# Awaiting the last stores behind the closing barrier instead of ahead of it

## The chip, the cores and the metric

The kernel runs on one core of a Trainium2 chip. The core has five engines that run their own instruction streams and meet only through semaphores: TensorE (PE), VectorE (DVE), ScalarE (ACT), GpSimd (POOL) and SyncE (SP), which issues most of the DMA transfers. The metric is device time in microseconds (us) of one execution. The profile of one execution gives a span, from its first to its last recorded instruction, beside the time of that same execution.

## The reference

The input is one sequence `x` of 2048 rows by 1024 columns in bfloat16. Two attention blocks are computed from it and mixed row by row by a gate:

```python
g = sigmoid((x * gate_w).sum(-1))
a = A(x, A_wqkv, A_wo)     # linear attention, 32 heads of 32: phi(q) (phi(k)^T v) / (phi(q) sum phi(k)), then @ wo
b = B(x, B_wqkv, B_wo)     # local attention: each row sees 8 rows back in steps of 2, softmax, then @ wo
out = g * a + (1 - g) * b
```

`phi(t)` is `t + 1` for positive `t`, otherwise `exp(t)`, plus 1e-6. Both blocks begin with a projection of 1024 to 3072 columns.

## The kernel before, in words

The kernel is written as a list of operations, each with an engine, a cost, the memory it reads and writes and a priority. A planner in `Prog.schedule` (line 122) orders them on each engine by these costs and priorities, and `Prog.emit` (line 208) turns the plan into the engines' instruction streams with the semaphore waits that the dependencies need. All matrix products run in tiles of 128 rows by 512 columns with eight accumulating steps. Projections for both blocks come first, then the local attention, the totals of the linear attention, and at last the output: for each tile `t` of 128 rows, `final(t)` (line 1736) multiplies block B's result with its output matrix on TensorE (line 1747), VectorE adds the gated result of block A (line 1751), and a DMA stores the tile (line 1757). Two output buffers, `o0` and `o1`, take turns.

The last tile is split into three column parts, 0 to 512, 512 to 768 and 768 to 1024. Each part is stored on its own: the first two by SyncE, the third by ScalarE. Each store raises a semaphore when its data has landed; which one follows from the buffer and the first column: `c_out0_0`, `c_out1_0`, `c_out1_512` and `c_out1_768`.

Near the end every engine runs `tail` (line 1820). It waits for a flag, computed on VectorE from the data (line 1798), which says whether the fast formulas are safe for this input; it loads the flag into a register (line 1823) and branches on it (line 1824). If the flag is 0, the engine finishes its planned operations, waits for everything, and then runs a second, general program (`general_path`), whose instructions stand in the stream between the branch and the other arm. If the flag is not 0, which is what happens with these inputs, the engine jumps to the other arm (line 1830). How much planned work lies behind the branch differs by engine: `BACK` keeps the last 19 us of the plan behind it on SyncE, 14 us on VectorE and 30 us on ScalarE; TensorE and GpSimd have none there and branch after all their work.

In that other arm SyncE, once its last stores are issued, waits for the completion semaphores that no later operation has waited for (`P.last`, line 260). They are the four named above. Then the arms join, and the block that holds all five streams closes at line 1836. Its close is a barrier: SyncE, ScalarE, TensorE and VectorE each execute a DRAIN, which counts the engine as arrived; GpSimd, having executed its own, waits for all four, and then lets every engine through with a second semaphore step. Behind the barrier nothing of the kernel follows.

Of the kernel before, what the change touches and what calls it, by code (L numbers as in the profile page):

```python
# [1116 lines left out]
def build_kernel(nc, A_x, A_wqkv, A_wo, B_x, B_wqkv, B_wo, gate_w, out):  # L1117
# [698 lines left out]
    P, flag_op = best[:2]  # L1816
# [3 lines left out]
    def tail(e, eng, rest):  # L1820
        reg = e.alloc_register("fast_ok")
        e.wait_ge(*flag_op.val)
        e.reg_load(reg, flag[0:1, 0:1])
        with e.If_eq(reg, 0):
            rest()
            for s, v in P.final + [(P.esem[x], n) for x, n in P.counts.items() if n]:
                e.wait_ge(s, v)
            for th in progs[eng]:
                th(e)
        with e.Else():  # L1830
            rest()
            if eng == "sp":
                for s, v in P.last:
                    e.wait_ge(s, v)

    with nc.Block() as block:
        P.emit(block, tail, flag_op)
    es_g.__exit__(None, None, None)
    return P


def bass_gated_mix__linear_attn_block__sliding_local_dilated__prompt_kernel(nc, A_x, A_wqkv, A_wo, B_x, B_wqkv, B_wo, gate_w, out):
    return build_kernel(nc, A_x, A_wqkv, A_wo, B_x, B_wqkv, B_wo, gate_w, out)
# [28 lines left out]
```

## Time and profile before

| | |
|---|---|
| median of 4 runs | 483.16 us (482.53 to 483.67) |
| the profiled execution's own time | 482.88 us |
| its span, first to last recorded instruction | 481.1 us |
| TensorE matmul busy | 471.4 us, 98% |
| VectorE busy | 281.3 us, 58% |
| ScalarE busy | 146.6 us, 30% |
| GpSimd busy | 6.2 us, 1% |
| granted TensorE clock | 1.000 |

A busy time counts computing instructions alone: register loads, branches, semaphore waits and the issuing of DMAs are not counted, and in answers on single lines they carry the engine's name with a q (SPq, PEldq). PE means matmuls, PEld the loads of their stationary operand. A releaser is what ended an engine's wait. A line with "x2" stands for two instructions. For a DMA, "us to landing" is counted from its issue to its semaphore. Answers on single lines give starts to a tenth of a microsecond; a narrower window places an instruction more closely.

### The profile page before, as it was taken

Reading aid. Unit: us, or ns where it says so; the run is one execution under the profiler, and the core shown is the slowest. Engines: PE = TensorE matmul, PEld = TensorE weight load, DVE = VectorE, ACT = ScalarE, POOL = GpSimd, SP = SyncE. Lnnn points to the kernel's source line nnn. Section 1 sums busy time; section 2 is a strip of 40 time slices with the busy share of each in tenths; the row PEclk is TensorE's granted clock in tenths of the full one; section 3 lists DMA queues with packets and bytes.
Section 4 is the critical chain, followed back from the end, with each engine's and each line's share of the span. In section 5 each row is a group of like instructions: output and inputs, shape, how many; then the busy total and the mean of one; then the engine's idle time right before and its main releaser. Section 6 shows DMA issues by size and latency. Waiting matters only on the chain.

```text
span 481.1 us, 10169 instructions
## 1 busy us (share of the span) xinstructions
PE 471.4 (98%) x4354; PEld 224.0 (47%) x4403; DVE 281.3 (58%) x578; ACT 146.6 (30%) x234; POOL 6.2 (1%) x38
## 2 busy tenths in 40 slices
PE   8999999999999999999999999999999999999997
PEld 3444444444444544545454455444444444444443
DVE  3212337888587788556737565597588136643434
ACT  2111111135333345435434335255542130111000
POOL 4000000000000000000000000000000000000000
PEclk9999999999999999999999999999999999999999
DMA  8999991132014337432313457720194019830212
GB/s 210 250 213 313 351 361 62 50 111 82 1 35 140 88 102 146 95 70 66 78 43 86 99 130 165 227 45 2 19 249 128 0 20 249 213 23 2 89 68 90
DMA packets 72951, 57.39 MB, mean 119 GB/s; under 512 B 37953, under 2 KB 60865, under 8 KB 72898
## 3 DMA queue, kind: packets, MB, share of 16 engines
q1 hardware_dynamic: 72210, 56.07, 44.4%
q8 instruction: 36, 0.59, 0.5%
q10 hardware_dynamic: 688, 0.59, 0.4%
q14 instruction: 17, 0.14, 0.1%
HBM read 34.49 MB, written 13.76 MB: 100 GB/s over the span
## 4 chain that ended last, share of the span: by engine, by line
PE 98%; issue 1%; DVE 0%
PE ps_all L1344 80%; PE ps_all L1747 11%; PE ps_all L1464 2%; PE ps_all L1499 2%; PE ps_all L1588 1%; PE ps_all L1383 1%; PE ps_all L1692 0%; PE ps_all L1664 0%; DVE o L1751 0%; DVE warm L1290 0%
## 5 line engine op out<-in xcount | busy, mean ns | idle before, releaser
L1344 PE MATMUL ps_all<-w,xT 128*128 128x512 bf16 x934 | 206.7, 379 | 3.1 <-issue 2.5
L1344 PE MATMUL ps_all<-xT,w 128*128 128x512 bf16 x750 | 165.6, 379 | 2.0 <-issue 1.6
L1344 PEld LDWEIGHTS ps_all<-w,xT 128*128 128x128 bf16 x960 | 92.3, 98 | 110.6 <-DMA xT<-in_A_x_dram 0.8
L1344 PEld LDWEIGHTS ps_all<-xT,w 128*128 128x128 bf16 x768 | 74.1, 98 | 89.5 <-issue 1.3
L1747 PE MATMUL ps_all<-w,qT 128*128 128x512 bf16 (+1 forms) x260 | 55.4, 372 | 0.2
L1747 PEld LDWEIGHTS ps_all<-w,qT 128*128 128x128 bf16 x264 | 25.8, 98 | 29.7
L1355 DVE TENSOR_SCALAR e<-e 128x512 bf16<-128x512 bf16 x64 | 18.6, 291 | 32.1 <-ACT e L1353 17.1
L1478 ACT ACTIVATE E<-ps_all 128x1824 bf16<-128x1824 f32 (+1 forms) x18 | 30.4, 1688 | 18.9 <-PE ps_all L1499 18.9
L1375 DVE CAST vst<-ps_all 128x512 bf16<-128x512 f32 x16 | 11.1, 694 | 41.7 <-PE ps_all L1344 41.7
L1751 DVE SCALAR_TENSOR_TENSOR o<-ps_all,gm,xT 128x512 bf16<-128x512 f32 (+1 forms) x25 | 18.0, 728 | 21.2 <-PE ps_all L1747 21.1
L1353 ACT ACTIVATE e<-ps_all 128x512 bf16<-128x512 f32 x32 | 19.1, 597 | 31.4 <-PE ps_all L1344 31.4
L1351 ACT ACTIVATE e<-ps_all 128x512 bf16<-128x512 f32 x32 | 19.1, 597 | 26.0 <-PE ps_all L1344 24.8
L1302 DVE TENSOR_TENSOR mx<-mx,kT 128x1024 bf16<-128x1024 bf16 x32 | 21.0, 687 | 9.1 <-ACT kT L1376 9.0
L1516 DVE TENSOR_TENSOR ot<-ps_all,rs 128x480 bf16<-128x480 f32 (+1 forms) x54 | 25.9, 507 | 0.0
L1302 DVE TENSOR_TENSOR mx<-mx,qT 128x1024 bf16<-128x1024 bf16 x32 | 21.1, 687 | 7.2 <-ACT qT L1379 7.1
L1376 ACT ACTIVATE az<-ps_all 128x512 bf16<-128x512 f32 x23 | 13.8, 600 | 36.3 <-PE ps_all L1344 36.3
L1376 ACT ACTIVATE vst<-ps_all 128x512 bf16<-128x512 f32 x16 | 9.6, 600 | 47.4 <-PE ps_all L1344 47.4
L1376 ACT ACTIVATE kT<-ps_all 128x512 bf16<-128x512 f32 x21 | 12.5, 597 | 36.8 <-PE ps_all L1344 36.8
L1379 ACT ACTIVATE qT<-ps_all 128x512 bf16<-128x512 f32 x19 | 11.3, 597 | 35.3 <-PE ps_all L1344 35.3
L1515 DVE RECIPROCAL rs<-ps_all 128x15 f32<-128x15 f32 (+1 forms) x54 | 9.4, 203 | 21.2 <-PE ps_all L1499 19.3
L1357 DVE SCALAR_TENSOR_TENSOR pk<-ps_all,e 128x512 bf16<-128x512 f32 x32 | 21.7, 680 | 0.1
L1379 ACT ACTIVATE xT<-ps_all,g 128x512 bf16<-128x512 f32 x10 | 6.9, 688 | 45.1 <-PE ps_all L1344 45.1
(73 smaller groups left out, 276.2 us busy)
## 6 DMA issues: line engine op xcount, KB each, us to landing
rb<-rc_hbm SPq DMA_DIRECT2D x32, 256.0 KB, 5.6
w<-in_A_wqkv_dram SPq DMA_DIRECT2D x6, 1024.0 KB, 9.1
v<-vB_hbm SPq DMA_DIRECT2D x36, 132.0 KB, 2.7
vB_hbm<-vst SPq DMA_DIRECT2D x32, 132.0 KB, 5.4
w<-in_B_wqkv_dram SPq DMA_DIRECT2D x4, 1024.0 KB, 8.3
xn<-in_A_x_dram SPq DMA_DIRECT2D x16, 256.0 KB, 2.7
out_dram<-o SPq DMA_DIRECT2D x15, 256.0 KB, 2.2
oB_hbm<-ot SPq DMA_DIRECT2D x36, 96.0 KB, 2.0
```

The lines of the kernel that those rows point to most:

```text
L1302: P.op("dve", lambda e, m=m, op=op: e.tensor_tensor(m[:, 0:n], m[:, 0:n], src, op), 0.08 + n / 1920.0, reads=[m.all(), reg], writes=[m.all()],
L1344: last = e.matmul(bank.ap(), lhs(dc), rhs(dc), start=(dc == 0), stop=(dc == 7))
L1351: P.op("act", lambda e: e.activation(e_[:, :], bank.ap(), ACT.Exp), act(512), reads=[bank.iv], writes=[e_.all()])
L1353: P.op("act", lambda e: e.activation(e_[:, :], bank.ap(), ACT.Exp, accum_out=qe[:, col:col + 1]), act(512) + 0.1, reads=[bank.iv], writes= ...
L1355: P.op("dve", lambda e: e.tensor_scalar(e_[:, :], e_[:, :], 1.0, 1e-6, op0=ALU.min, op1=ALU.add), 0.25, reads=[e_.all()], writes=[e_.all()])
L1357: P.op("dve", lambda e: e.scalar_tensor_tensor(out=dst, in0=bank.ap(), scalar=0.0, in1=e_[:, :], op0=ALU.max, op1=ALU.add), dps(512), read ...
L1376: fa = lambda e: e.activation(dst, src(), ACT.Copy)
L1379: fa = lambda e: e.activation(dst, src(), ACT.Copy, scale=scale)
L1478: P.op("act", lambda e: e.activation(E[:, 0:32 * nq].rearrange("p (j q) -> p j q", j=4), ps[:, 4:8, 0:8 * nq], ACT.Exp), act(32 * nq), rea ...
L1516: P.op("dve", lambda e, r=r, src=src, dst=dst, m=m: e.tensor_tensor(dst, src()[:, :, 0:32], r[:, 0:m, None].to_broadcast([128, m, 32]), AL ...
L1747: last = e.matmul(bank.ap(0, f1 - f0), qT[:, dc, t * 128:(t + 1) * 128], ws[3][:, dc, f0:f1], start=(dc == 0), stop=(dc == 7))
L1751: P.op("dve", lambda e, bank=bank, o_=o_, t=t, n=n, i0=i0, i1=i1, tgt=tgt, c0=c0: e.scalar_tensor_tensor(out=o_[:, i0 * 128:i1 * 128].rear ...
```

## The change

Three lines leave the arm of the conditional in which SyncE waits for the completion of the last stores, and two lines with the same waits come after the block has closed. Those waits are still executed by SyncE alone. The block's close, and so the barrier, comes ahead of them in SyncE's stream.

```diff
         with e.Else():
             rest()
-            if eng == "sp":
-                for s, v in P.last:
-                    e.wait_ge(s, v)
 
     with nc.Block() as block:
         P.emit(block, tail, flag_op)
+    for s, v in P.last:
+        nc.sync.wait_ge(s, v)
     es_g.__exit__(None, None, None)
     return P
```

In the built program SyncE's four waits take two event-wait instructions and the wait of a branch before the change, and two event-wait instructions after it, two semaphores to each. The streams of the other four engines hold the same instructions in the same order.

## The prediction

> **What bounds the kernel now.** I read three things in order: the chain that ended last (what sets the span), then its last stretch in order of time, then every instruction of the lines that the change touches.
>
> The page's chain, by engine, and the chain's end by time (start, length, what):
>
> ```profile
> PE 98%; issue 1%; DVE 0%
> ```
>
> ```profile
> 469.81 8.24 PE ps_all L1747 x46
> 478.04 0.02 issue
> 478.07 0.48 DVE o L1751
> ```
>
> TensorE carries the kernel to 478.04 us, one VectorE addition to 478.55, and there the chain stops. The span is 481.1, so 481.1 - 478.55 = 2.6 us stand behind the last computation. No page row charges them to anybody; only the queue entries of the single lines show them. The change lies wholly inside these 2.6 us.
>
> The last three stores, as the DMA issues between 477 and 480 us (size, us to landing), and what SyncE waited for from 475 us on (total, times, longest):
>
> ```profile
> out_dram<-o SPq DMA_DIRECT2D x1, 128.0 KB, 2.7
> out_dram<-o SPq DMA_DIRECT2D x1, 64.0 KB, 2.9
> out_dram<-o ACTq DMA_DIRECT2D x1, 64.0 KB, 1.8
> ...
> SPq L1834 <- DMA out_dram<-o: 1.6, 1, 1.6
> ```
>
> The 64 KB store that SyncE issues at 477.7 takes 2.9 us to land: 480.6. ScalarE's, issued at 478.58, is there at 478.6 + 1.8 = 480.4. SyncE's own issue lasts 1.25 us, to 478.96, and from then it waits 1.6 us for a landing.
>
> Then each instruction of the touched lines (count, ns min/median/max, first and last start):
>
> ```profile
> L1824 PEldq COMPARE_BRANCH  x1: 3744/3744/3744, 476.3 to 476.3; - x1
> ...
> L1834 SPq EVENT_SEMAPHORE  x2: 17/22/28, 480.6 to 480.7; - x2
> ...
> L1830 SPq COMPARE_BRANCH  x1: 37/37/37, 480.7 to 480.7; - x1
> ...
> L1836 POOLq EVENT_SEMAPHORE  x2: 17/17/17, 481.0 to 481.0; - x2
> L1836 POOLq DRAIN  x1: 114/114/114, 433.8 to 433.8; - x1
> L1836 DVEq DRAIN  x1: 524/524/524, 478.1 to 478.1; - x1
> L1836 ACTq DRAIN  x1: 152/152/152, 479.0 to 479.0; - x1
> L1836 PEldq DRAIN  x1: 73/73/73, 480.1 to 480.1; - x1
> L1836 SPq DRAIN  x1: 13/13/13, 480.9 to 480.9; - x1
> L1836 SPq EVENT_SEMAPHORE  x1: 17/17/17, 481.1 to 481.1; - x1
> ```
>
> Line 1836 is the closing barrier. Each engine arrives with its DRAIN: GpSimd at 433.8, VectorE at 478.1 (done 478.60), ScalarE 479.0, TensorE 480.1, SyncE last at 480.9. GpSimd collects the arrivals and releases all. By narrowing the window to hundredths I place SyncE's steps: first wait of line 1834 at 480.60 to 480.61, second at 480.67 to 480.68, branch (line 1830) at 480.74 to 480.75, DRAIN at 480.91 to 480.92, GpSimd's two steps at 480.95 to 480.96 and 481.03 to 481.04, SyncE through the release at 481.08 to 481.09. So today the order is landing, then waits, branch and barrier, one after another. The surprise is TensorE: its last matmul starts at 477.76 and its arrival is 480.06, because its branch on the flag takes 3.7 us, from 476.26 to 480.01.
>
> **What the Trainium skill says.** "Perfetto Trace Analysis", section Sequencer-only Instruction (DRAIN, etc): the recorded time is the execution alone; the wait ahead of it and the spread of the semaphore behind it are not recorded. The trace agrees: entries of 13 to 28 ns stand 43 to 170 ns apart, so I price steps from start to start. The same page, section DMA Instruction — HWDGE (DVE, Sync): the semaphore of a store is written only after its last data write is confirmed, which can take surprisingly long into HBM; here ScalarE's 64 KB take 1.8 us. "Runtime: NRT & Kernel Launch", section Instruction fetch mechanics: a taken branch whose target isn't in the loaded window waits for a fetch. TensorE's 3.7 us branch agrees: the trace has a 16 KB instruction packet between 477.5 and 477.6 us, inside it. The same page, section The ~15µs preamble/postamble breakdown: behind the kernel the runtime has all engines wait for one another again. No view here shows that part; I use it only to say who ends the run.
>
> **The change part by part.**
>
> *Removed:* two event waits and a wait carried by the branch, in SyncE's branch of the conditional. Four completion semaphores are awaited: both output buffers and the two halves of the last tile.
>
> *Added:* the same four in two event waits behind the barrier, on SyncE alone. No matmul, vector operation or transfer changes, and the order of all engines' instructions is otherwise the same. Until the last store's issue ends at 478.96 nothing can differ, so the first 479 us cost zero, with no cover needed.
>
> *Moved, step 1: SyncE arrives early.* After 478.96 it has only its branch and DRAIN left, 480.745 to 480.925 today, some 0.2 us. It arrives near 479.2 instead of 480.92. The DRAIN might wait for transfers in flight; ScalarE's says no: at 479.0 it took 0.15 us, with its own store landing at 480.4.
>
> *Step 2: the barrier now waits for TensorE.* Arrivals: VectorE 478.60, ScalarE 479.15, SyncE 479.2, TensorE 480.06 + 0.07 = 480.14. From the last arrival to SyncE's release takes 481.085 - 480.925 = 0.16 us today, so release at 480.30, and SyncE stands at its first wait by about 480.35.
>
> *Step 3: the waits end as today.* The landing shows at 480.605; the second wait starts 0.07 us later and lasts 0.03: done at 480.70. Queued behind the waits on SyncE is only the program's end, and no other engine waits for it. The barrier is thus hidden under the store's landing with 480.605 - 480.35 = 0.25 us to spare. Without that cover (TensorE 0.25 us or more later) the gain shrinks by every further microsecond of lateness.
>
> *Sum.* The last record falls from 481.14 (TensorE's release, 481.09 + 0.05) to 480.70: -0.44 us, made of branch, DRAIN and barrier passage leaving the path. The other four engines are released at 480.3 instead of 481.1: -0.8, of use only if one of them, not SyncE, decides the run's end.
>
> The profiled execution took 482.88 us for a span of 481.1; 1.78 us lie around it. I assume they stay: 480.70 + 1.78 = 482.48 (481.14 + 1.74 before). The median of the four runs is 483.16, 0.28 above the profiled one, so against it 483.16 - 0.44 = 482.7.
>
> *Unknown cost:* what the runtime does in the 1.78 us. Lower end: nothing gained, if the end hangs on something unmoved. Upper end: 0.8, if it hangs on the four released engines. A loss isn't excluded by this either; it is bounded below. I take 0.44, because SyncE is last to finish on both sides and an end that waits for all engines waits for it.
>
> **The rivals.**
>
> *The end is set elsewhere: no change, 483.16.* For: the trace still has an instruction packet of 16 KB between 480.7 and 480.8, of the same queue as TensorE's, so an engine may be fetching its closing code whatever SyncE does. Against: it begins before today's release and nothing shows anybody waiting for it.
>
> *The four released engines decide: -0.8, 482.4.* For: TensorE's stream is the slowest at the end already. Against: SyncE's last wait would have to end nothing.
>
> *A little slower: TensorE arrives last.* If its branch took not 3.7 but over 4.5 us, it would arrive after 480.9, where SyncE arrives today. Then the barrier ends at the same moment in both kernels, and the changed one has the two event waits still to run behind it: 2 x 0.07 = 0.14 us, giving 483.3. It decides from a TensorE arrival about 0.8 us later than seen; between 0.25 and 0.6 the gain shrinks through zero. Only one execution shows the branch, so its spread is unknown.
>
> *Much slower: SyncE's new waits fall on code not yet fetched.* A stall like TensorE's 3.7 us would give up to 486.4 when nothing hides it. Against: SyncE's branch at 459.1 is followed by two 8 KB instruction packets by 462.5, which already hold the arm and its end; the next two on that queue, between 463 and 477, come after VectorE's own branch at 464.8. SyncE's stream hardly changes length.
>
> *It doesn't do what it says:* stores that land ahead of the barrier's end would leave waits of zero, and SyncE's release would again be the last record. The 0.25 us above speak against it.
>
> **How the numbers follow.** Chances: the forecast (0.44 gained) 0.58, no change 0.17 (the last rival included), 0.8 gained 0.14, a little slower 0.07, much slower 0.04. A measurement of this kernel can tell about 0.2% from no change, 0.97 us: under 482.2 or over 484.1. No mechanism above gains that much; the largest, 482.4, is 0.2 short, and the four runs alone scatter from 482.53 to 483.67, so a little of the two gaining cases spills over: faster 0.15. Slower takes the stall and a trace of scatter: 0.05. The rest, 0.80, is within. The range for 8 in 10 takes in 482.4, 483.16 and 483.3, with some 0.4 of scatter at the low end and 0.2 at the high one, where cases are rarer: 482.0 to 483.5. The stall is left out.
>
> **What would show it.** Right: SyncE's DRAIN near 479.2; TensorE's the last arrival, near 480.1; GpSimd's two steps near 480.2; SyncE's release before its event waits, and those at 480.6 and 480.7 as the last records; a span of 480.7. Step 1 is wrong if SyncE's DRAIN lasts until 480.4 or more; step 2 if another engine's arrival is last; step 3 if the release comes after the landing. A span of 480.7 with an unchanged run time says that the end is set outside the span. A second long branch, or an instruction packet ahead of SyncE's waits, would make the forecast wrong.

## The result, and the profile after

The changed kernel takes 482.42 us in the median of 40 runs (481.76 to 483.05), the kernel before 482.96 us in 60 runs. The ratio is 0.9988, with a 95% interval of 0.9983 to 0.9992: 0.58 us faster, between 0.39 and 0.82. The forecast was 482.7 us, 0.44 us faster than the 483.16 it started from.

The single profiled executions hide this: 482.77 us after against 482.88 before, and a span of 481.1 us in both. The chain's end tells why (start, length, what):

```profile
3 pieces in order of time: start us, us, what
473.85 4.78 PE ps_all L1747 x30
478.63 0.02 issue
478.65 0.48 DVE o L1751
```

The last addition ends at 479.14 us, where it ended at 478.55 before: this one execution reached the tail 0.59 us later. That lies in the 478 us that the change does not touch, and within the scatter: the runs of one kernel lie some 1.3 us apart. Behind the last addition the kernel before needed 2.59 us to its last record and 4.33 to the end of the run; the changed one needed 2.01 and 3.63. What is to be compared is the tail, and across runs, not the two spans.

The closing barrier of the changed kernel is on line 1833, its waits on line 1836. Each entry is count, ns min/median/max, first and last start:

```profile
L1824 PEldq COMPARE_BRANCH  x1: 3824/3824/3824, 476.8 to 476.8; - x1
...
L1833 POOLq EVENT_SEMAPHORE  x2: 17/17/17, 480.8 to 480.9; - x2
...
L1833 DVEq DRAIN  x1: 524/524/524, 478.7 to 478.7; - x1
L1833 SPq DRAIN  x1: 127/127/127, 478.7 to 478.7; - x1
L1833 ACTq DRAIN  x1: 152/152/152, 479.6 to 479.6; - x1
L1833 PEldq DRAIN  x1: 73/73/73, 480.7 to 480.7; - x1
L1833 SPq EVENT_SEMAPHORE  x1: 17/17/17, 481.0 to 481.0; - x1
...
L1836 SPq EVENT_SEMAPHORE  x2: 27/28/28, 481.1 to 481.1; - x2
```

SyncE now arrives at 478.7, before ScalarE and TensorE, and TensorE is the last at 480.7 because of its 3.8 us branch. Narrower windows give release at 480.97, the first wait at 481.06 and the second at 481.12. And SyncE's waits of this stretch (total, times, longest), with the stores' landing below:

```profile
SPq L1757 <- DVE o L1751: 4.7, 3, 3.1
SPq L1833 <- PEq L1833: 2.2, 1, 2.2
```

```profile
out_dram<-o SPq DMA_DIRECT2D x1, 128.0 KB, 2.8
out_dram<-o SPq DMA_DIRECT2D x1, 64.0 KB, 2.3
out_dram<-o ACTq DMA_DIRECT2D x1, 64.0 KB, 1.6
```

SyncE waits 2.2 us for TensorE at the barrier and not at all for a landing: SyncE's last store, issued at 478.29, landed at 480.6, ScalarE's at 480.8, both before the release. Before, the wait for the landing (1.6 us) stood in this list, and the wait at the barrier was this:

```profile
SPq L1836 <- PEq L1836: 0.2, 1, 0.2
```

SyncE's last store was issued faster here (0.33 us) than in the execution before (1.25 us) and landed earlier. The gain doesn't come from that: in a_late1 below, which runs the changed kernel's instructions again, the issue took 1.22 us, and the run's end stands 3.52 us behind the last addition.

Each run also has its own span, so its time splits into the span and what lies outside. Over 42 runs of the changed kernel the span is 480.87 us on average and the rest 1.59; over 48 runs of the kernel before, beside the first experiments, 481.33 and 1.74. So 0.45 us came from the span and 0.16 from outside it. The forecast had left the second part unchanged. Why it shrank is the question for the experiments.

### The profile page after: what moved, and what is told of

Read it like the earlier page. It is cut to its first block, busy times and chain, and to the rows that moved or that the text cites. A ratio compares the mean times of both kernels' runs of the same rounds, so it can differ in the third digit from the quotient of the medians.

```text
span 481.1 us, 10168 instructions
## 1 busy us (share of the span) xinstructions
PE 472.0 (98%) x4354; PEld 224.3 (47%) x4403; DVE 281.5 (59%) x578; ACT 146.6 (30%) x234; POOL 6.2 (1%) x38
## 4 chain that ended last, share of the span: by engine, by line
PE 98%; issue 1%; DVE 0%
PE ps_all L1344 80%; PE ps_all L1747 11%; PE ps_all L1464 2%; PE ps_all L1499 2%; PE ps_all L1383 1%; PE ps_all L1588 1%; PE ps_all L1692 0%; PE ps_all L1664 0%; DVE o L1751 0%; DVE warm L1290 0%
```

## The experiments

A name with b_ is an edit of the kernel before, one with a_ an edit of the changed kernel. All ratios are to the kernel before, run on the same chip in the same job. Rows of different jobs are compared by their ratios rather than by their medians: a_near and a_late1 are of the first job, a_sp10, a_sp30 and a_pew of the second, a_early and a_all of the third, and the changed kernel of its own measurement above. "Outside" is the mean over a kernel's runs of its time less its span.

| kernel | median us | ratio, 95% interval | mean span | outside |
|---|---|---|---|---|
| before (three jobs) | 483.06, 482.95, 483.05 | 1 | 481.33, 481.27, 481.29 | 1.74, 1.74, 1.75 |
| changed | 482.42 | 0.9988, 0.9983 to 0.9992 | 480.87 | 1.59 |
| b_near | 483.50 | 1.0007, 1.0001 to 1.0014 | 481.72 | 1.75 |
| a_near | 482.31 | 0.9985, 0.9977 to 0.9994 | 481.03 | 1.25 |
| b_late1 | 483.20 | 1.0000, 0.9991 to 1.0008 | 481.35 | 1.74 |
| a_late1 | 482.43 | 0.9990, 0.9982 to 0.9998 | 480.95 | 1.59 |
| a_sp10 | 482.41 | 0.9990, 0.9983 to 0.9996 | 481.15 | 1.31 |
| a_sp30 | 482.96 | 0.9996, 0.9988 to 1.0005 | 481.72 | 1.25 |
| a_pew | 483.23 | 1.0005, 0.9997 to 1.0013 | 481.55 | 1.66 |
| b_pew | 483.18 | 1.0004, 0.9996 to 1.0013 | 481.42 | 1.76 |
| a_early | 481.97 | 0.9981, 0.9974 to 0.9988 | 480.63 | 1.48 |
| b_early | 482.94 | 0.9994, 0.9986 to 1.0003 | 481.05 | 1.75 |
| a_all | 482.65 | 0.9994, 0.9986 to 1.0003 | 481.03 | 1.72 |

### TensorE's long branch made short

In both kernels TensorE's part of the general program, the arm that these inputs do not take, is left out, so that its jump is short:

```diff
+    progs["pe"] = []
+
     def tail(e, eng, rest):
```

> The kernel before, with TensorE's part of the second, general program left out (the arm that these inputs do not take), so that TensorE's branch is a short jump. Theory 1 (before the change the landing of the last stores sets the end, and TensorE's arrival at the barrier has some 0.8 us to spare): no change, within 0.1 us; TensorE's DRAIN near 0.1 us after its last matmul instead of 2 us. Rival 2 (TensorE's long branch is on the path in both kernels): 0.3 us or more faster than before. Rival 3 (the run's end hangs on TensorE's own closing code, not on SyncE): more than 0.5 us faster, with an unchanged span.

> The changed kernel with the same part left out: TensorE's jump is short. Theory 1 (after the change TensorE's arrival is the last, and holds SyncE ahead of waits that are already satisfied): the barrier is passed near 0.9 us after the last VectorE operation, SyncE then waits for the landing, and the time falls by 0.2 to 0.3 us below the changed kernel's, to about 0.8 us below before. Rival 2, the forecast as recorded (TensorE has 0.25 us to spare, the landing sets the end): the same time as the changed kernel, 0.5 us below before. Rival 3 (the released engines decide): 1 us or more below the changed kernel.

The changed kernel with the short jump, branch, barrier and waits:

```profile
L1826 PEldq COMPARE_BRANCH  x1: 358/358/358, 476.3 to 476.3; - x1
...
L1835 PEldq DRAIN  x1: 1398/1398/1398, 476.7 to 476.7; - x1
...
L1835 ACTq DRAIN  x1: 152/152/152, 479.1 to 479.1; - x1
L1835 SPq DRAIN  x1: 137/137/137, 479.1 to 479.1; - x1
L1835 SPq EVENT_SEMAPHORE  x1: 17/17/17, 479.4 to 479.4; - x1
...
L1838 SPq EVENT_SEMAPHORE  x2: 28/28/28, 480.8 to 480.8; - x2
```

TensorE's arrival is done with its last matmul, at 478.1; SyncE and ScalarE are the last. The release moves to 479.38, and SyncE then waits for the landing until 480.75, 1.3 us. So the release came about 1 us earlier against the last addition, yet the median moves only 0.1 us below the changed kernel, less than the 0.2 to 0.3 expected, and the intervals do not tell the two apart. SyncE's wait explains part: its last record stands 2.22 us behind the last addition, 0.2 later than in the changed kernel. But the part outside the span fell from 1.59 to 1.25, far beyond its scatter between runs (standard deviations of 0.03 to 0.10 us). SyncE's last wait can't be what the run's end always follows.

The kernel before did not gain from the short jump, so TensorE wasn't on its path. But it came out 0.3 to 0.4 us slower, where no change within 0.1 was expected, and its interval just leaves out 1. Its part outside is unchanged and its tail, 2.53 us, is no longer than before's. The difference isn't explained.

### More time for TensorE, in a form that leaves no second instruction

A second load of the flag was written into TensorE's stream:

```diff
-        e.reg_load(reg, flag[0:1, 0:1])
+        for _ in range(2 if eng == "pe" else 1):
+            e.reg_load(reg, flag[0:1, 0:1])
```

> The kernel before, with one more load of the flag register on TensorE ahead of its branch (0.49 us by the profile). Theory 1: TensorE's arrival moves by 0.5 us inside its 0.8 us of cover: no change, within 0.1 us. Rival 2 (TensorE is on the path before the change): 0.5 us slower.

> The changed kernel with the same additional load on TensorE. Theory 1: TensorE is last at the barrier, so the whole 0.5 us is paid: 0.5 us above the changed kernel, which is level with before. Rival 2 (0.25 us of cover): 0.25 us above the changed kernel. Rival 3: as theory 1 in time, but the span's part behind SyncE's last wait would grow too.

The built program and the trace hold one load, not two; the first one's register would have been overwritten unread. So nothing of the expectations was tested, and these are repeats of the two kernels. As such they agree: 1.0000 and 0.9990, with 1.74 and 1.59 outside. Their profiles show how close the two conditions lie in the changed kernel. In a_late1 SyncE is released at 480.37, finds its first wait satisfied, and starts the second at 480.59, held up 0.07 us by ScalarE's store, which has landed at 480.58.

### Time added on SyncE alone

From a_near I formed a fourth theory: the run's end is the later of two, a fixed time behind the release of the other engines or a shorter fixed time behind SyncE's last record. More satisfied waits on SyncE, behind the barrier, move the second and leave the first:

```diff
     for s, v in P.last:
         nc.sync.wait_ge(s, v)
+    for s, v in P.final[:10]:      # 30 in a_sp30
+        nc.sync.wait_ge(s, v)
```

> The changed kernel with 10 more waits on long satisfied semaphores on SyncE, after its own two, as five instructions of some 0.065 us each: SyncE ends 0.3 us later, nobody else does. Theory 4, formed from the first runs (the run ends at the later of two: the other engines' release + 1.74 us, or SyncE's last wait + 1.25 us; in the changed kernel the first is later by 0.3 to 0.4): the same time as the changed kernel within 0.1 us, the span 0.3 us longer, and the part of the run outside the span 0.3 us shorter, near 1.3. Theory 1 as recorded in the forecast (SyncE's last wait decides, a fixed 1.6 to 1.8 us lies around the span): 0.3 us slower than the changed kernel, the part outside unchanged.

> The same with 30 waits, 15 instructions: SyncE ends 1.0 us later. Theory 4: the first 0.35 us are free, the rest is paid: 0.6 us slower than the changed kernel, which is level with before, with the part outside the span at its floor of 1.25 us. Theory 1: 1.0 us slower than the changed kernel, 0.4 above before, the part outside unchanged near 1.6.

The waits as the traces have them, ten and thirty added:

```profile
L1838 SPq EVENT_SEMAPHORE  x7: 28/28/28, 480.7 to 481.1; - x7
```

```profile
L1838 SPq EVENT_SEMAPHORE  x17: 28/28/28, 481.0 to 481.9; - x17
```

Five more instructions, 0.06 us apart, make SyncE end 0.3 us later: 482.41 against 482.42 us, nothing. The mean span grew by 0.28 and the part outside shrank by 0.28. With fifteen, SyncE ends 0.9 us later, the time rises by 0.54 us in the median (0.4 by the ratios, whose intervals overlap), and the part outside stops at 1.25. The part outside, which scatters by 0.04 us or less in these two kernels, is the sharper measure: it fell from 1.59 to 1.25 and no further, so some 0.35 us of SyncE's closing were free. This contradicts the forecast's assumption that SyncE decides the end, and agrees with the fourth theory on both sides of its corner.

### Time added on TensorE

Five instructions with satisfied waits stand between TensorE's branch and the barrier:

```diff
         with e.Else():
             rest()
+            if eng == "pe":
+                for s, v in P.final[:10]:
+                    e.wait_ge(s, v)
```

> The changed kernel with five more instructions on TensorE between its branch and the closing barrier, 10 waits on long satisfied semaphores; by the 51 ns of one such instruction on TensorE 0.3 to 0.6 us later at the barrier (the trace tells). Theory 4: the release, and with it the run's end, moves by the whole of it: 0.3 to 0.6 us slower than the changed kernel. Theory of the forecast (0.25 us of cover, SyncE's landing decides): 0.05 to 0.35 slower. If TensorE's arrival does not matter: no change.

> The kernel before with the same five instructions on TensorE. Theory 4 and the forecast alike: TensorE has some 0.8 us to spare ahead of SyncE at the barrier, so no change, within 0.1 us. If TensorE were on the path before the change: as much slower as the changed kernel is by the same edit.

The changed kernel with the edit:

```profile
L1834 PEldq EVENT_SEMAPHORE  x5: 51/51/51, 480.5 to 480.9; - x5
...
L1830 PEldq COMPARE_BRANCH  x1: 193/193/193, 481.1 to 481.1; - x1
...
L1836 PEldq DRAIN  x1: 8/8/8, 481.3 to 481.3; - x1
L1836 SPq EVENT_SEMAPHORE  x1: 17/17/17, 481.5 to 481.5; - x1
...
L1839 SPq EVENT_SEMAPHORE  x2: 28/28/28, 481.6 to 481.6; - x2
```

Behind the five waits TensorE also executes a branch out of the arm (line 1830), so the edit costs it more than expected: its arrival is complete 2.36 us behind the last addition instead of 1.67, 0.69 us later. The changed kernel pays all of it: 483.23, 0.81 above the 482.42 without it. The kernel before has TensorE's arrival now 0.06 us behind SyncE's (both at 480.8 to 480.9), so the slack of some 0.8 us that the first profile showed is used up:

```profile
L1839 SPq DRAIN  x1: 13/13/13, 480.8 to 480.8; - x1
L1839 PEldq DRAIN  x1: 8/8/8, 480.9 to 480.9; - x1
```

It comes out 0.23 us above in the median, and its interval includes no change. The two kernels cannot be told apart, 483.23 and 483.18. This is the rival in which TensorE arrives last, brought about by an edit: once TensorE arrives as late as SyncE did, the change gains nothing.

### The load of the flag moved ahead, nothing left out

If the release of the other engines is the bound, TensorE's arrival should be brought forward. Its load of the flag, 0.49 us, can run while earlier matmuls are still queued:

```diff
     def run(e, eng):
...
+            if eng == "pe":
+                go(e, ops[:k - 2])
+                tail(e, eng, lambda: None, lambda: go(e, ops[k - 2:]))
+                return
...
         e.reg_load(reg, flag[0:1, 0:1])
+        between()      # on TensorE: its last two matmul groups
```

> The changed kernel with TensorE's load of the flag (0.49 us) moved ahead of its last two matmul groups, so that its branch can start when the last matmul has been handed on; nothing is left out. Theory 4: TensorE reaches the barrier 0.5 us earlier, the other engines are released 0.5 us earlier, and the run's end follows until SyncE's own waits + 1.25 us decide: 0.15 to 0.35 us faster than the changed kernel, 0.7 to 0.9 below before, with the part outside the span falling from 1.6 to 1.25 to 1.4. Theory of the forecast (the landing decides already): the same time as the changed kernel.

> The kernel before with the same move. TensorE is not the last at the barrier here; theory 4 and the forecast: no change, within 0.1 us. It also tells whether the earlier load holds up the last matmuls: then it would be slower by up to 0.5 us.

The changed kernel with the edit, branch, barrier and waits:

```profile
L1829 PEldq COMPARE_BRANCH  x1: 3864/3864/3864, 476.0 to 476.0; - x1
...
L1838 PEldq DRAIN  x1: 8/8/8, 480.0 to 480.0; - x1
L1838 SPq EVENT_SEMAPHORE  x1: 17/17/17, 480.2 to 480.2; - x1
...
L1841 SPq EVENT_SEMAPHORE  x2: 28/28/28, 480.3 to 480.5; - x2
```

The branch starts 2.8 us before the end of the last addition instead of 2.3; TensorE's arrival is complete 1.16 us behind it instead of 1.67. The release follows, at 480.18, and SyncE then does wait for a landing: its second wait is over at 480.54. The result is 481.97 us, 0.9981 of before, the fastest of all. Against the changed kernel's 0.9988 that is 0.34 us less, within the 0.15 to 0.35 expected; the medians lie 0.45 apart, but they are of different jobs. The two intervals, 0.9974 to 0.9988 and 0.9983 to 0.9992, overlap, so the step between the two is likely rather than proved. The part outside fell from 1.59 to 1.48, less far than the 1.25 to 1.4 expected. The kernel before has the same edit without a difference that its interval tells, and its last 184 matmuls aren't held up by it: 38.02 us, as in b_pew without the edit.

### All five engines wait for the landing

```diff
     for s, v in P.last:
-        nc.sync.wait_ge(s, v)
+        for e in (nc.sync, nc.scalar, nc.tensor, nc.vector, nc.gpsimd):
+            e.wait_ge(s, v)
```

> The changed kernel with the four waits behind the barrier executed by all five engines, not by SyncE alone. Theory 4: the other four engines end later by two waits (2 x 0.106 us on TensorE, by the added waits of the earlier run) or with the landing, and the run with them: 0.2 us slower than the changed kernel, 0.35 below before, the part outside the span back at 1.7. If SyncE alone decided the end: the same time as the changed kernel.

```profile
L1837 POOLq EVENT_SEMAPHORE  x2: 42/42/43, 480.7 to 480.8; - x2
L1837 SPq EVENT_SEMAPHORE  x2: 27/28/28, 480.8 to 480.8; - x2
L1837 ACTq EVENT_SEMAPHORE  x2: 38/38/38, 480.8 to 480.8; - x2
L1837 DVEq EVENT_SEMAPHORE  x2: 50/50/50, 480.8 to 480.9; - x2
L1837 PEldq EVENT_SEMAPHORE  x2: 51/51/51, 480.8 to 480.9; - x2
```

482.65 us, 0.23 above the changed kernel (0.3 by the ratios, whose intervals overlap), with 1.72 outside: as the fourth theory had it, to the extent that a difference of this size can be told. The part outside, which scatters little, is the clearer sign: it is back where it was before the change as soon as the other engines end as late as SyncE.

### The two bounds in the profiled executions

Each profiled execution has its own time, and narrower windows place its last records to a hundredth. "Release" is the start of ScalarE's step through the barrier; "SyncE" the start of its last record. (The 1.74 and 1.25 us of the expectations are counted from the ends of the last records, of TensorE and SyncE; these here are counted from starts and so are a little longer.)

| execution | time us | release | time less release | SyncE | time less SyncE |
|---|---|---|---|---|---|
| before | 482.88 | 481.09 | **1.79** | 481.08 | 1.80 |
| changed | 482.77 | 480.98 | **1.79** | 481.12 | 1.65 |
| a_late1 | 482.17 | 480.38 | **1.79** | 480.59 | 1.58 |
| a_early | 481.97 | 480.18 | **1.79** | 480.54 | 1.43 |
| a_pew | 483.27 | 481.49 | **1.78** | 481.63 | 1.64 |
| a_sp10 | 482.43 | 480.65 | **1.78** | 481.10 | 1.33 |
| a_near | 482.09 | 479.39 | 2.70 | 480.81 | **1.28** |
| a_sp30 | 483.20 | 480.87 | 2.33 | 481.92 | **1.28** |

Six executions end 1.78 to 1.79 us behind the release, whatever SyncE does in between; in the two where SyncE is more than 0.5 us behind the release, the end is 1.28 us behind SyncE. The difference of the two numbers, 0.5 us, is the time that SyncE's waits may take for nothing.

In the four edits of the kernel before, SyncE's last record is its own step through the barrier, as in before itself. Their executions end 1.79 (b_near, b_pew), 1.80 (b_early) and 1.85 us (b_late1) behind the release. The 0.06 us by which b_late1 is off are not explained. In a_all, where the other engines have two more waits each behind the barrier, the end is 1.97 us behind the release.

## Why the prediction was right or wrong

**The sum.** 0.44 us was forecast, 0.58 measured (0.39 to 0.82). The sign held, and the size lies near the low end of the interval; that it lies inside is in part luck. The 0.44 is the shift of the last record, from 481.14 to 480.70, with everything behind it left as it was. By the two bounds of the table, the forecast's own release at 480.30 and its last wait at 480.67 would give the later of 482.09 and 481.95 us, 0.79 below the 482.88 of that execution. In the profile after, the release came 0.09 us later behind the last addition than forecast (1.84 us, not 1.75), and the run's end moved with it, by 0.70 us. A small slip is in the sum: 1.78 belongs to the rounded span of 481.1; with the 1.74 that belongs to 481.14 the profiled execution's forecast is 482.44, not 482.48. The 482.7 doesn't rest on it.

**Step 1, SyncE arrives early: right.** Its DRAIN is at 478.7 after (479.1 in a_near and a_late1, 479.2 forecast) and lasts 0.13 us with its stores in flight. That a DRAIN doesn't wait for transfers was read correctly from ScalarE's.

**Step 2, the barrier waits for TensorE: right.** TensorE's DRAIN is the last arrival, 1.67 us behind the last addition (1.59 before), and from there to SyncE's release it took 0.17 us (0.16 forecast).

**Step 3, the waits end with the landing, 0.25 us of cover: wrong as a rule.** The release came after the landing, which the forecast itself had named as the sign. In the profile after, both stores had landed 0.2 to 0.4 us before the release, and the waits took no time but their own 0.06 us steps. In the repeat a_late1 one wait was over 0.07 us late. The cover was the difference of two small numbers from one execution. One of them hung on SyncE's last store, whose issue took 1.25 us there and 0.33 us in the changed kernel's execution, with a landing 2.9 and 2.3 us behind its start. The forecast had seen the 1.25 and taken it for fixed.

**"I assume they stay: 480.70 + 1.78": this is the step that failed.** The part outside the span fell from 1.74 to 1.59. The reason given, "SyncE is last to finish on both sides and an end that waits for all engines waits for it", doesn't follow: the end stands 1.79 us behind the release of the other engines but only 1.28 behind SyncE's last record, so SyncE may come up to 0.5 us after they are released without moving the end. The forecast put this difference at nothing. What the prediction took from the Trainium skill, "Runtime: NRT & Kernel Launch", section The ~15µs preamble/postamble breakdown, that all engines wait for one another behind the kernel, agrees with an end that is the later of two; that the two distances differ by 0.5 us only the runs showed. a_sp10 shows the free time, and a_sp30 where it ends.

**The rival "the four released engines decide" was right in its mechanism**, at a chance of 0.14. Its 0.8 us was the shift of the release, 481.1 to 480.3, taken from one execution. The release moved by 0.70 us between the two profiles (2.54 to 1.84 us behind the last addition); 0.8 lies at the end of the measured interval and 0.7 well inside. The argument against it, "SyncE's last wait would have to end nothing", was what happens in the changed kernel.

**The rival "TensorE arrives last: a little slower".** Its mechanism was shown by a_pew: with TensorE 0.69 us later the gain is gone. A net loss of 0.14 us was not: the ratio to before is 1.0005 and its interval holds 1, and against b_pew there is no difference. By the table it should not exist, since two waits on SyncE are inside its 0.5 us.

**The rival "it doesn't do what it says" had its premise right.** The stores did land ahead of the barrier's end, against the forecast's 0.25 us, and the waits found nothing to wait for. The conclusion, no change, was wrong: the release itself came 0.70 us earlier, since SyncE no longer reached the barrier behind the landing.

**The other two rivals fell.** The end is not set by something unmoved: it moves with the release. And SyncE's new waits did not stall: the first starts 0.09 us behind its release and the second 0.06 us later. What the forecast said against that rival, that two instruction packets "already hold the arm and its end", no view shows.

**What stays open.** Which of the other four engines decides, and what they do in the time behind the barrier, which no view shows. In all kernels but a_all they pass the barrier within 0.05 us of one another. In a_all their last records end apart, and the run's end is 1.77 us behind ScalarE's (1.78 in the kernel before), but 1.66 behind TensorE's (1.74), 1.70 behind VectorE's (1.77) and 1.79 behind GpSimd's (1.82). That points weakly at ScalarE: it is one execution, and b_late1 was off by 0.06 us without a known reason. Open also is b_near's loss of 0.3 to 0.4 us. A kernel without any wait for its last stores would price the waits themselves; it wasn't tried, since its output could be read before it has landed.

## What to carry to other kernels

Put the wait for the last stores behind the closing barrier, on one engine: the barrier's passage, and what the other engines do behind it, then run while the stores land. What bounded the end here after that was mostly the last engine to arrive, so look for an engine that reaches the barrier late for a reason that nobody counts as busy, here a long branch, and take out of its way what can be done earlier, as the load of the flag here. For an edit of half a microsecond compare the tail behind the last computation and split each run's time into span and rest; two spans from one execution each may show nothing.

## What the runs showed of the hardware

In the profiled executions the run's end is 1.78 to 1.80 us behind the moment in which the barrier lets the other engines go (1.85 in one of ten), or 1.28 us behind the start of SyncE's last instruction, whichever is later; the profile's span shows neither. An instruction that waits for two satisfied semaphores costs 0.06 us on SyncE and 0.106 us on TensorE, start to start. An explicit DRAIN on SyncE took 0.13 us and one on ScalarE 0.15 us while stores that these engines had issued were still on their way. The issue of one and the same 64 KB store on SyncE took 0.33 us in some executions and 1.2 to 1.4 in others, with landings 2.3 us and 2.6 to 3.0 us behind its start (0.8 and 0.9 us in a_early and b_early). The changed kernel and its three edits that add waits only behind the barrier on SyncE or on all engines had 0.33 us; a_late1, the changed kernel repeated, had 1.22, so no run here tells what decides it. TensorE's branch over its part of the other arm took 3.7 to 4.0 us in every execution, and 0.36 us when that part was left out.
